# Second product of a two-layer FFN kernel: low part of the squares as stationary weights, in short 64-row pairs woven between the long passes, with five sum banks

## The chip, the cores and the metric

One core of a Trainium2 chip runs the whole problem. The metric is the device time of one execution in microseconds; less is better. The kernel before takes 2247.69 us (median of 2 runs, 2247.62 to 2247.77).

## The reference

A short dynamic convolution per head is followed by a squared-ReLU feed-forward layer. `x` is 8 x 4096 x 192, the heads are 8 of 24 columns, the convolution has 7 taps, the hidden width is 2048, and all arrays are float32 (the FFN's weights arrive as float64 and the kernel decodes them).

```python
w = softmax(weight_gen)                       # over the 7 taps
y = einsum('bshk,bskhg->bshg', w, x_unfolded) # 32768 tokens x 192
h = y @ w_in                                  # 192 x 2048
g = maximum(h, 0) ** 2
out = g @ w_out                               # 2048 x 192
```

## The kernel before

The 32768 tokens are cut into 64 chunks of 512 (`NCH`, 4 tokens for each of 128 partitions). For each chunk VectorE computes softmax and taps (L211, L216), transposes (L270), and DMAs over a DRAM scratch tile turn the result into `xT`, three groups of 64 rows, which stand twice, in partitions 0 to 63 and 64 to 127. ScalarE casts a high part `xh` (L235), VectorE subtracts it for the low part `xl` (L236). Both products use a split of each operand into a high and a low part in the round float format `F32R`; the product of the two low parts is left out.

The 2048 hidden columns are 16 blocks of 128, taken in pairs: a *step* `(c, j)` handles blocks 2j and 2j+1 of chunk c, 8 steps a chunk. In a step TensorE first makes the first product (`mm1`, L300): nine passes, each a *pair* of matmuls, one in rows 0 to 63 and one in rows 64 to 127 of the array, weights 64x128, 512 token columns moving, into two PSUM tiles `ph` of a pool of four. ScalarE then does relu (L316) and square (L320) of both blocks, and at the step's end casts their high parts `gh` (L324). VectorE subtracts for the low parts `gl` (L328) in the *next* step, ahead of that step's other VectorE work (the list `late`). TensorE's second product for a block pair (`mm2_turned`, L372) comes two steps after its first product (`LAG = 2`), behind the nine passes of that step: ten pairs, weights from `V` (the high and low parts of `w_out`), `gh` or `gl` moving with 512 columns, into four sum banks `acc` that hold the output turned: output columns on partitions, tokens along the free axis. The output's columns 0 to 127 use two banks, columns 128 to 191 the other two.

When a chunk's last block pair is summed, `sum_turned` (in step 1 of the next chunk) copies two banks on ScalarE (L380), adds the other two on VectorE (L382) and moves 64 rows by DMA (L383). `store_turned` turns the sums back: part 0 in step 5 (VectorE transpose L391, then 16 DMAs into `o_sb`, L400), part 1 in step 6 (an add L393, a transpose L394, 8 DMAs L400, then the store to DRAM, L405). All DMAs are issued on SyncE's queue, in program order.

The order of work on each engine is the order in which the code is written (`manual_schedule`); a table `todo` spreads the VectorE work of the next convolution over the steps, and the casts and low parts of the next chunk's `x` lie in step 6. The first chunk (c = 0) and the last have code of their own; in the last one `mm2` (L336, L345) uses the squares as weights, 128 tokens at a time. Chunks 1 to 62 go through `mm2_turned`.

Of the kernel before, what the change touches and what calls it, by code (L numbers as in the profile page):

```python
# [8 lines left out]
F32 = mybir.dt.float32  # L9
# [3 lines left out]
ALU = mybir.AluOpType  # L13
# [6 lines left out]
def kernel(  # L20
# [9 lines left out]
    nc = tc.nc  # L30
    B, S, D = x.shape
# [3 lines left out]
    P = 128  # L35
    Q = 32
# [3 lines left out]
    TC = 4  # L40
    NCH = n_chunks or R // TC
    TG = 8
    CPG = TG // TC
    NF = FF // P
    D1 = 64
    ND = D // D1
    N = TC * P
    NJ = NF // 2
    NU = NJ // 2
    WI = ND * P  # L50
    N_PE = 2
    LAG = 2
    CONV_BEG = 3
    OUT_STEP = 5
# [3 lines left out]
    stage = ctx.enter_context(tc.tile_pool(name="stage", bufs=3))  # L58
# [3 lines left out]
    gp = ctx.enter_context(tc.tile_pool(name="gp", bufs=NBUF))  # L62
    op = ctx.enter_context(tc.tile_pool(name="op", bufs=1))
    dram = ctx.enter_context(tc.tile_pool(name="dram", bufs=2, space=bass.MemoryType.DRAM))
    ps_h = ctx.enter_context(tc.tile_pool(name="ps_h", bufs=4, space=bass.MemoryType.PSUM))
    ps_o = ctx.enter_context(tc.tile_pool(name="ps_o", bufs=1, space=bass.MemoryType.PSUM))

    x_v = x.rearrange("b s d -> (b s) d").rearrange("(p r) d -> p r d", r=R)
# [1 line left out]
    out_v = out.rearrange("(p r) d -> p r d", r=R)  # L70
# [5 lines left out]
    W = const.tile([P, 2, NJ, WI], F32R, name="W")  # L76
    V = const.tile([P, NF, 2 * D], F32R, name="V")
# [207 lines left out]

    phs, rgs, ghs, gls, accs = {}, {}, {}, {}, {}

    def mm1(c, j, parts=(0, 1)):
        xh, xl = xts[c]["h"], xts[c]["l"]
        if 0 in parts:  # L290
            phs[c, 2 * j], phs[c, 2 * j + 1] = [ps_h.tile([P, N], F32, name="ph") for _ in range(2)]
        two = phs[c, 2 * j], phs[c, 2 * j + 1]
        seq = [(q, xx, k) for q, xx in ((0, xh), (0, xl), (1, xh)) for k in range(ND)]
        for n, (q, xx, k) in enumerate(seq):
            if q not in parts:
                continue
            for i in range(2):
                rows = slice(i * D1, (i + 1) * D1)
                w = W[rows, q, j, k * P:(k + 1) * P]
                nc.tensor.matmul(two[i], w, xx[rows, k], start=(n == 0), stop=(n == len(seq) - 1))  # L300

    def relu(c, fb):
        ph = phs.pop((c, fb))
# [14 lines left out]
    def square(c, fb):  # L318
        r = rgs[c, fb]
        nc.scalar.activation(r, r, AF.Square)  # L320
# [4 lines left out]

    def low(c, fb):
        gl = gls[c, fb] = gp.tile([P, N], F32R, name="gl")
        nc.vector.tensor_tensor(out=gl, in0=rgs.pop((c, fb)), in1=ghs[c, fb].bitcast(F32), op=ALU.subtract)  # L328

    def mm2_tile(c, fb, t):  # L330
        acc = accs[c][t]
# [23 lines left out]
            del ghs[c, fb], gls[c, fb]  # L355


    def mm2_turned(c, fb):
        if fb == 0:
            accs[c] = [ps_o.tile([P, N], F32, name=f"acc{t}") for t in range(4)]  # L360
        gh, gl = ghs.pop((c, fb)), gls.pop((c, fb))
        j, i = divmod(fb, 2)
        first, last = fb == 0, fb == NF - 1
        A, B = [(0, 0, gh), (0, 0, gl), (0, 1, gh)], [(2, None, gh), (2, None, gl)]
        seq = B + A if last or first else A + B
        for n, (b, q, g) in enumerate(seq):
            k = sum(1 for m in seq[:n] if m[0] == b)
            for h in range(2):
                rows = slice(h * D1, (h + 1) * D1)
                w = V[rows, fb, P:2 * P] if q is None else V[rows, fb, 2 * P * q:2 * P * q + P]  # L370
                fl = dict(start=first and k == 0, stop=last and k == (2 if b == 0 else 1))
                nc.tensor.matmul(accs[c][b + h], w, g[rows], **fl)  # L372

    works = {}

    def sum_turned(c):
        acc = accs[c]
        X = works[c] = stage.tile([P, 3, N], F32, name="raw")
        for k, b in ((1, 2), (0, 0)):
            nc.scalar.copy(X[:, k], acc[b])  # L380
        for k, b in ((1, 2), (0, 0)):
            nc.vector.tensor_tensor(out=X[:, k], in0=acc[b + 1], in1=X[:, k], op=ALU.add)  # L382
        nc.sync.dma_start(out=X[0:D1, 2], in_=X[D1:P, 1])  # L383

    def store_turned(c, part):
        X = works[c]
        if part == 0:
            o_sb = op.tile([P, TC, D], F32, name="o_sb", bufs=2)
            Y = stage.tile([P, 2, N], F32, name="raw")
            outs[c] = o_sb, Y  # L390
            nc.vector.transpose(Y[:, 0], X[:, 0])  # L391
        else:
            nc.vector.tensor_tensor(out=X[0:D1, 1], in0=X[0:D1, 1], in1=X[0:D1, 2], op=ALU.add)  # L393
            nc.vector.transpose(outs[c][1][0:D1, 1], X[0:D1, 1])  # L394
        o_sb, Y = outs[c]
        y = Y[:, part].rearrange("p (t q i) -> p q t i" if c < N_PE else "p (q t i) -> p q t i", t=TC, i=Q)
        for e in range(P // Q if part == 0 else D1 // Q):
            d0 = part * P + e * Q
            for q in range(P // Q):
                nc.sync.dma_start(  # L400
                    out=o_sb[q * Q:(q + 1) * Q, :, d0:d0 + Q],
                    in_=y[e * Q:(e + 1) * Q, q],
                )
        if part:
            nc.sync.dma_start(out=out_v[:, c * TC:(c + 1) * TC, :], in_=o_sb)  # L405

    outs = {}

# [43 lines left out]
    for u in range(NU):  # L452
# [11 lines left out]
        fbs = [4 * u + i for i in range(4)]  # L464
# [60 lines left out]
    for c in range(1, NCH):  # L525
        tail = c == NCH - 1
        for j in range(NJ):
            if j == 0 and c % 2 and (c + 3) // 2 * CPG < NCH:
                load_group((c + 3) // 2)
            if j == CONV_BEG and c + 2 < NCH:  # L530
                plan_conv(c + 2, *conv_steps(c + 2, 0))
            if c == 1 and j == 0:
                for t in range(TC):
                    finish(0, t)
                store(0, 0, TC)
            mm1(c, j)
            fbs = (2 * j, 2 * j + 1)
            done = None
            if len(pend) == LAG or tail and pend:
                c2, j2 = pend.pop(0)  # L540
                for fb in (2 * j2, 2 * j2 + 1):
                    mm2_turned(c2, fb)
                done = c2 if j2 == NJ - 1 else None
            for fb in fbs:
                relu(c, fb)
            for fb in fbs:
                square(c, fb)
            if not tail:
                pend.append((c, j))
            for f in late:  # L550
                f()
            late.clear()
            if done is not None:
                sum_turned(done)
            for f in todo.pop((c, j), []):
                f()
            if c > 1 and j == OUT_STEP:
                store_turned(c - 1, 0)
            if c > 1 and j == OUT_STEP + 1:
                store_turned(c - 1, 1)  # L560
            if not tail or j < NJ // 2:
                for fb in fbs:
                    high(c, fb)
                    late.append(lambda c=c, fb=fb: low(c, fb))
    c = NCH - 1
# [43 lines left out]
```

## Time and profile before

| | |
|---|---|
| runs | 2247.62 and 2247.77 us |
| span of the profiled execution | 2246.2 us |
| TensorE busy | 2228.7 us, 99% |
| weight loads busy | 1846.4 us, 82% |
| VectorE busy | 1877.6 us, 84% |
| ScalarE busy | 1797.6 us, 80% |
| GpSimd busy | 1.7 us |
| DMA | 191.78 MB, 85 GB/s |

In the profile, PE is TensorE's matmuls and PEld its weight loads, DVE is VectorE, ACT ScalarE, POOL GpSimd, SP or SPq the queue of SyncE that issues DMAs. A row of a timeline has the start in us, the time in us, engine, line, operation, output and inputs, shape, and in brackets how long the engine had been idle and what ended that. A row of a group has the count, the busy time, the mean of one in ns, and the idle time before. In the rows by windows each engine has busy us and, in brackets, its instructions, in the order PE, PEld, DVE, ACT, POOL; then come the granted TensorE clock, the DMA share and GB/s.

### The profile page before, as it was taken

The page shows a single profiled execution, that of the slowest core. Times are in us where ns is not written, and L with a number is a line of the kernel's source. Part 1 is how long each engine was busy: PE and PEld are TensorE (multiplying, and loading weights), DVE is VectorE, ACT ScalarE, POOL GpSimd, SP SyncE. Part 2 cuts the span into 40 slices and gives each one's busy share as a digit, 9 for nine tenths or more (in the row PEclk, how much of TensorE's full clock was granted, in tenths as well). Part 3 has the DMA queues.
Part 4 walks back from the last instruction along what each step waited for, and adds up shares of the span by engine and source line. Part 5 has one row for each costly group of instructions (what it writes and reads, how often), then busy time and mean ns, then how long its engine had stood idle before and what let it go on. Part 6 is the DMA issues. An engine that isn't in the chain of part 4 may idle for free.

```text
span 2246.2 us, 50242 instructions
## 1 busy us (share of the span) xinstructions
PE 2228.7 (99%) x19632; PEld 1846.4 (82%) x19632; DVE 1877.6 (84%) x2834; ACT 1797.6 (80%) x3462; POOL 1.7 (0%) x7
## 2 busy tenths in 40 slices
PE   7999999999999999999999999999999999999999
PEld 7788888888888888888888888888888888888887
DVE  8988888888888888888888888888888889888884
ACT  5688888888888888888888888888888888888876
POOL 0000000000000000000000000000000000000000
PEclk9999999999999999999999999999999999999999
DMA  5233233332333332333323333323333233332321
GB/s 170 60 91 90 58 99 85 91 100 67 80 94 81 100 88 59 99 84 93 99 54 93 88 88 99 83 65 100 84 91 90 57 99 86 91 99 71 76 66 45
DMA packets 321390, 191.78 MB, mean 85 GB/s; under 512 B 223752, under 2 KB 280968, under 8 KB 317184
## 3 DMA queue, kind: packets, MB, share of 16 engines
q1 hardware_dynamic: 321152, 188.58, 33.5%
q8 instruction: 153, 2.51, 0.5%
q14 instruction: 85, 0.70, 0.1%
HBM read 106.39 MB, written 49.55 MB: 69 GB/s over the span
## 4 chain that ended last, share of the span: by engine, by line
PE 97%; DVE 1%; ACT 1%; DMA 0%; issue 0%; SPq 0%; DVEq 0%; ACTq 0%
PE acc L372 49%; PE ph L300 45%; PE acc L336 1%; PE acc L345 1%; PE ph L253 1%; DVE pr L211 0%; DVE pr L216 0%; DMA xt<-in_x_dram 0%; ACT rg L320 0%; ACT gh L324 0%; DVE gl L328 0%; DMA raw<-in_moe_w_in_dram 0%; DVE V L156 0%; ACT rg L316 0%; ACT rg L310 0%
## 5 line engine op out<-in xcount | busy, mean ns | idle before, releaser
L372 PE MATMUL acc<-gh,V 64*128 64x512 f32 x5952 | 1007.5, 386 | 0.7 <-ACT gh L324 0.7
L300 PE MATMUL ph<-xh,W 64*128 64x512 f32 x6144 | 863.8, 386 | 2.0 <-ACT W L148 1.8
L316 ACT ACTIVATE rg<-ph 128x512 f32<-128x512 f32 x992 | 539.2, 597 | 346.9 <-PE ph L300 346.9
L372 PE MATMUL acc<-gl,V 64*128 64x512 f32 x3968 | 772.8, 386 | 1.0 <-DVE gl L328 1.0
L328 DVE TENSOR_TENSOR gl<-rg,gh 128x512 fp32r<-128x512 f32 x1008 | 644.4, 679 | 147.5 <-ACT gh L324 147.4
L300 PEld LDWEIGHTS ph<-xh,W 64*128 64x128 f32 x6144 | 575.8, 184 | 125.8 <-ACT W L148 3.0
L372 PEld LDWEIGHTS acc<-gh,V 64*128 64x128 f32 x5952 | 557.5, 184 | 118.1 <-ACT gh L324 1.1
L320 ACT ACTIVATE rg<-rg 128x512 f32<-128x512 f32 x1008 | 581.8, 634 | 0.0
L324 ACT CAST gh<-rg 128x512 fp32r<-128x512 f32 x1008 | 576.4, 627 | 2.6 <-PE acc L345 2.6
L372 PEld LDWEIGHTS acc<-gl,V 64*128 64x128 f32 x3968 | 371.7, 184 | 80.1 <-DVE gl L328 2.1
L300 PE MATMUL ph<-xl,W 64*128 64x512 f32 x3072 | 432.3, 386 | 0.0
L211 DVE TENSOR_TENSOR pr<-xt,wt 128x768 f32<-128x768 f32 x448 | 420.0, 950 | 3.4 <-DMA xt<-in_x_dram 1.2
L216 DVE TENSOR_TENSOR pr<-pr 128x768 f32<-128x768 f32 x381 | 361.5, 949 | 0.3
L300 PEld LDWEIGHTS ph<-xl,W 64*128 64x128 f32 x3072 | 288.3, 184 | 60.8 <-DVE xl L236 0.4
L236 DVE TENSOR_TENSOR xl<-xT,xh 128x512 fp32r<-128x512 f32 x186 | 117.7, 688 | 185.2 <-ACT xh L235 185.2
L235 ACT CAST xh<-xT 128x512 fp32r<-128x512 f32 x186 | 102.7, 625 | 0.0
L382 DVE TENSOR_TENSOR raw<-acc,raw 128x512 f32<-128x512 f32 x124 | 79.9, 686 | 3.0 <-ACT raw L380 3.0
L197 ACT ACTIVATE wt<-wt 128x224 f32<-128x224 f32 x64 | 25.0, 391 | 65.1 <-DVE wt L196 65.1
L380 ACT COPY raw<-acc 128x512 f32<-128x512 f32 x124 | 66.6, 598 | 0.0
L270 DVE STREAM_TRANSPOSE xr<-pr 128x768 f32<-128x768 f32 x62 | 60.7, 979 | 2.1
L394 DVE STREAM_TRANSPOSE raw<-raw 64x512 f32<-64x512 f32 x62 | 43.6, 704 | 2.1
L391 DVE STREAM_TRANSPOSE raw<-raw 128x512 f32<-128x512 f32 x62 | 43.7, 705 | 0.0
(46 smaller groups left out, 393.5 us busy)
## 6 DMA issues: line engine op xcount, KB each, us to landing
xT<-xd SPq DMA_DIRECT2D x124, 384.0 KB, 4.9
xt<-in_x_dram SPq DMA_DIRECT2D x31, 1344.0 KB, 7.0
out_dram<-o_sb SPq DMA_DIRECT2D x63, 384.0 KB, 2.7
xd<-xr SPq DMA_DIRECT2D x248, 96.0 KB, 2.0
o_sb<-raw SPq DMA_DIRECT2D x1488, 16.0 KB, 1.8
raw<-raw SPq DMA_DIRECT2D x62, 128.0 KB, 4.1
wt<-in_weight_gen_dram SPq DMA_DIRECT2D x31, 224.0 KB, 3.2
raw<-in_moe_w_in_dram SPq DMA_DIRECT2D x16, 192.0 KB, 4.1
```

What stands on the lines that cost most here:

```text
L211: tt(out=dst, in0=src, in1=wk.broadcast_to([P, n, G]), op=ALU.mult)
L216: tt(out=prs[k0], in0=prs[k0], in1=prs.pop(k), op=ALU.add)
L235: nc.scalar.copy(xh, src[k])
L236: tt(out=xl, in0=src[k], in1=xh.bitcast(F32), op=ALU.subtract)
L300: nc.tensor.matmul(two[i], w, xx[rows, k], start=(n == 0), stop=(n == len(seq) - 1))
L316: nc.scalar.activation(r, ph, AF.Relu)
L320: nc.scalar.activation(r, r, AF.Square)
L324: nc.scalar.copy(gh, rgs[c, fb])
L328: nc.vector.tensor_tensor(out=gl, in0=rgs.pop((c, fb)), in1=ghs[c, fb].bitcast(F32), op=ALU.subtract)
L372: nc.tensor.matmul(accs[c][b + h], w, g[rows], **fl)
L380: nc.scalar.copy(X[:, k], acc[b])
L382: nc.vector.tensor_tensor(out=X[:, k], in0=acc[b + 1], in1=X[:, k], op=ALU.add)
```

## The change

The second product of a block pair is now made of two kinds of pairs. Six *long* pairs keep `V` as weights and `gh` moving with 512 columns. The product of `gl` and the high part of `w_out` becomes eight *short* pairs: `gl` gives the weights, 128 tokens (64x128) at a time, and 192 columns of `V` move. Their sums are not turned (tokens on partitions) and get two banks of their own, `tx` and `ty`; the long pairs use three (`a0`, `a1`, `bb`). Five sum banks leave three for `ph`, in place of four; in the first chunk every second step takes the fifth sum bank for its second `ph` tile. The low parts are written with their tokens reordered so that blocks of 128 fit.

The short pairs are woven into the step's list of 15 long pairs (9 of the first product, 6 of the second): after the long passes number 2, 3, 5, 6, 10, 11, 13 and 14 (`SLOTS` has other places for a chunk's first and last block pair). Since the two row halves write the same banks at different times of a step, two orders per step are passed on through GpSimd: a no-op there waits for the one half's last matmul, and the other half's next matmul waits for the no-op.

The chunk's sum copies `tx` on VectorE and `a0`, `bb` and `ty` on ScalarE and needs one add less; the low sums are kept in `lows`. A third part of `store_turned`, in step 7, adds `lows` to `o_sb` on VectorE and then issues the store, which stood in part 1 before.

The places in the order of work. VectorE, from the transposes of step 6 to the low parts that step 0 of the next chunk makes (`gl` low parts, `pr` taps, `o_sb` the turned output), before:

```order
L394 STREAM_TRANSPOSE raw<-raw 64x512 [waits DVE_49]
L328 TENSOR_TENSOR gl<-rg,gh 128x512 [waits PE_49,Activation_49] x2
L211 TENSOR_TENSOR pr<-xt,wt 128x768
L216 TENSOR_TENSOR pr<-pr 128x768
L211 TENSOR_TENSOR pr<-xt,wt 128x768
L328 TENSOR_TENSOR gl<-rg,gh 128x512 [waits PE_49,Activation_49] x2
```

and now:

```order
L476 STREAM_TRANSPOSE raw<-raw 64x512 [waits DVE_49]
L341 TENSOR_TENSOR gl<-rg,gh 128x4x4x32 [waits PE_49,Activation_49] x2
L211 TENSOR_TENSOR pr<-xt,wt 128x768
L216 TENSOR_TENSOR pr<-pr 128x768
L211 TENSOR_TENSOR pr<-xt,wt 128x768
L466 TENSOR_TENSOR o_sb<-o_sb,lows 128x768 [waits DMAHW4_49,DMAHW5_49,DMAHW3_49,DMAHW6_49,DMAHW2_49,DMAHW7_49,DMAHW1_49,DMAHW0_49]
L341 TENSOR_TENSOR gl<-rg,gh 128x4x4x32 [waits PE_49,Activation_49] x2
```

The first pair of `gl` rows is block pair 6, the second block pair 7. The add of L466, which waits for DMAs, stands between them.

TensorE, in a chunk's step 1, which reads the low parts of the last chunk's block pair 7, before (the first product's passes, then the first rows of the second product; the numbers name the banks):

```order
L300 MATMUL ph<-xh,W 128x512 [waits Activation_49] x2
L300 MATMUL ph<-xh,W 128x512 x4
L300 MATMUL ph<-xl,W 128x512 x6
L300 MATMUL ph<-xh,W 128x512 x6
L372 MATMUL acc_15883<-gh,V 128x512 [waits Activation_49]
L372 MATMUL acc_15884<-gh,V 128x512
L372 MATMUL acc_15883<-gl,V 128x512 [waits DVE_49]
```

and now:

```order
L302 MATMUL ph<-xh,W 128x512 [waits Activation_49] x2
L302 MATMUL ph<-xh,W 128x512 x2
L423 MATMUL acc_17701<-V,gl 128x192 [waits DVE_49]
L423 MATMUL acc_17700<-V,gl 128x192
L302 MATMUL ph<-xh,W 128x512 x2
L423 MATMUL acc_17701<-V,gl 128x192
L423 MATMUL acc_17700<-V,gl 128x192
L302 MATMUL ph<-xl,W 128x512 x2
```

The first wait for VectorE's low part has moved from behind nine pairs of the first product to behind two; in the steps of block pairs 1 to 6 it stands behind three.

The diff:

```diff
--- before.py
+++ after.py
@@ -62,7 +62,7 @@
     gp = ctx.enter_context(tc.tile_pool(name="gp", bufs=NBUF))
     op = ctx.enter_context(tc.tile_pool(name="op", bufs=1))
     dram = ctx.enter_context(tc.tile_pool(name="dram", bufs=2, space=bass.MemoryType.DRAM))
-    ps_h = ctx.enter_context(tc.tile_pool(name="ps_h", bufs=4, space=bass.MemoryType.PSUM))
+    ps_h = ctx.enter_context(tc.tile_pool(name="ps_h", bufs=3, space=bass.MemoryType.PSUM))
     ps_o = ctx.enter_context(tc.tile_pool(name="ps_o", bufs=1, space=bass.MemoryType.PSUM))
 
     x_v = x.rearrange("b s d -> (b s) d").rearrange("(p r) d -> p r d", r=R)
@@ -285,19 +285,28 @@
 
     phs, rgs, ghs, gls, accs = {}, {}, {}, {}, {}
 
-    def mm1(c, j, parts=(0, 1)):
+    def mm1_passes(c, j, parts=(0, 1)):
         xh, xl = xts[c]["h"], xts[c]["l"]
         if 0 in parts:
-            phs[c, 2 * j], phs[c, 2 * j + 1] = [ps_h.tile([P, N], F32, name="ph") for _ in range(2)]
+            phs[c, 2 * j] = ps_h.tile([P, N], F32, name="ph")
+            phs[c, 2 * j + 1] = (ps_o.tile([P, N], F32, name="acc4") if c == 0 and j % 2
+                                 else ps_h.tile([P, N], F32, name="ph"))
         two = phs[c, 2 * j], phs[c, 2 * j + 1]
         seq = [(q, xx, k) for q, xx in ((0, xh), (0, xl), (1, xh)) for k in range(ND)]
-        for n, (q, xx, k) in enumerate(seq):
-            if q not in parts:
-                continue
-            for i in range(2):
-                rows = slice(i * D1, (i + 1) * D1)
-                w = W[rows, q, j, k * P:(k + 1) * P]
-                nc.tensor.matmul(two[i], w, xx[rows, k], start=(n == 0), stop=(n == len(seq) - 1))
+
+        def one(n, q, xx, k):
+            def f():
+                for i in range(2):
+                    rows = slice(i * D1, (i + 1) * D1)
+                    w = W[rows, q, j, k * P:(k + 1) * P]
+                    nc.tensor.matmul(two[i], w, xx[rows, k], start=(n == 0), stop=(n == len(seq) - 1))
+            return f
+
+        return [one(n, q, xx, k) for n, (q, xx, k) in enumerate(seq) if q in parts]
+
+    def mm1(c, j, parts=(0, 1)):
+        for f in mm1_passes(c, j, parts):
+            f()
 
     def relu(c, fb):
         ph = phs.pop((c, fb))
@@ -325,7 +334,11 @@
 
     def low(c, fb):
         gl = gls[c, fb] = gp.tile([P, N], F32R, name="gl")
-        nc.vector.tensor_tensor(out=gl, in0=rgs.pop((c, fb)), in1=ghs[c, fb].bitcast(F32), op=ALU.subtract)
+        ga, gb, to = rgs.pop((c, fb)), ghs[c, fb].bitcast(F32), gl
+        if N_PE <= c < NCH - 1:
+            ga, gb = [g.rearrange("p (q t j) -> p q t j", q=P // Q, j=Q) for g in (ga, gb)]
+            to = gl.rearrange("p (t q j) -> p q t j", q=P // Q, j=Q)
+        nc.vector.tensor_tensor(out=to, in0=ga, in1=gb, op=ALU.subtract)
 
     def mm2_tile(c, fb, t):
         acc = accs[c][t]
@@ -355,35 +368,104 @@
             del ghs[c, fb], gls[c, fb]
 
 
-    def mm2_turned(c, fb):
...
+    relay = {}
+
+    def waits_for(late_one, early_one):
+        tc.add_manual_dep(
+            late_one.ins, early_one.ins.name,
+            mybir.DependencyInfo(mybir.DependencyClass.Sync, mybir.DependencyReason.DATA),
+            reason="the other half of the rows has written this bank",
+        )
+
+    def passed_on(kind, last_one=None, next_one=None):
+        if last_one is not None:
+            relay[kind] = nc.gpsimd.engine_nop()
+            waits_for(relay[kind], last_one)
+        if next_one is not None:
+            waits_for(next_one, relay.pop(kind))
+
+    def mm2_passes(c, j):
+        if j == 0:
+            accs[c] = [ps_o.tile([P, N], F32, name=f"acc{b}") for b in range(5)]
+        a0, a1, bb, tx, ty = accs[c]
+        fbs = (2 * j, 2 * j + 1)
+        hs = [ghs.pop((c, fb)) for fb in fbs]
+        ls = [gls.pop((c, fb)) for fb in fbs]
+        turn = j % 2
+        last_b, last_t = [], []
+
+        def wide(kind, i):
+            fb, g = fbs[i], hs[i]
+            first, last = fb == 0, fb == NF - 1
+
+            def f():
+                to = {0: ((a0, 0), (bb, P)), 1: ((a0, 2 * P), (a1, 2 * P)), 2: ((bb, P), (a1, 0))}[kind]
+                for h, (b, col) in enumerate(to):
+                    rows = slice(h * D1, (h + 1) * D1)
+                    start = first and kind == (1 if b is a1 else 0)
+                    stop = last and kind == (1 if b is a1 else 0)
+                    m = nc.tensor.matmul(b, V[rows, fb, col:col + P], g[rows], start=start, stop=stop)
+                    if b is bb:
+                        last_b.append(m)
+                        if len(last_b) == 2:
+                            passed_on("side", last_one=m)
+                        if len(last_b) == 3:
+                            passed_on("side", next_one=m)
+            return f
+
+        def narrow(swap, i, t):
+            fb, g = fbs[i], ls[i]
+
+            def f():
+                for h in range(2):
+                    rows = slice(h * D1, (h + 1) * D1)
+                    b, tok = (tx, t) if h == swap else (ty, 2 + t)
+                    m = nc.tensor.matmul(
+                        b[:, t * D:(t + 1) * D], g[rows, tok * P:(tok + 1) * P], V[rows, fb, 0:D],
+                        start=fb == 0 and t == 0 and swap == 0, stop=fb == NF - 1 and t == 1 and swap == 0,
+                    )
+                    last_t.append(m)
+                    if len(last_t) == 8:
+                        passed_on("low", last_one=m)
+                    if len(last_t) == 9:
+                        passed_on("low", next_one=m)
+            return f
+
+        kinds, swaps = ((0, 1, 2), (0, 1)) if not turn else ((2, 1, 0), (1, 0))
+        return ([wide(k, i) for k in kinds for i in range(2)],
+                [narrow(w, i, t) for w in swaps for i in range(2) for t in range(2)])
+
+    SLOTS = {0: (9, 9, 10, 10, 13, 14, 14, 14), NJ - 1: (1, 2, 3, 4, 8, 9, 10, 11)}
+
+    def woven(wide, narrow, slots):
+        for n, f in enumerate(wide):
+            f()
+            for i, g in enumerate(narrow):
+                if slots[i] == n:
+                    g()
 
     works = {}
 
     def sum_turned(c):
-        acc = accs[c]
-        X = works[c] = stage.tile([P, 3, N], F32, name="raw")
-        for k, b in ((1, 2), (0, 0)):
-            nc.scalar.copy(X[:, k], acc[b])
-        for k, b in ((1, 2), (0, 0)):
-            nc.vector.tensor_tensor(out=X[:, k], in0=acc[b + 1], in1=X[:, k], op=ALU.add)
+        a0, a1, bb, tx, ty = accs[c]
+        X = stage.tile([P, 3, N], F32, name="raw")
+        L = op.tile([P, TC, D], F32, name="lows")
+        works[c] = X, L
+        lf = L.rearrange("p (b t) d -> p b (t d)", b=2)
+        nc.vector.tensor_copy(lf[:, 0], tx[:, 0:2 * D])
+        nc.scalar.copy(X[:, 0], a0)
+        nc.scalar.copy(X[:, 1], bb)
+        nc.scalar.copy(lf[:, 1], ty[:, 0:2 * D])
+        nc.vector.tensor_tensor(out=X[:, 0], in0=a1, in1=X[:, 0], op=ALU.add)
         nc.sync.dma_start(out=X[0:D1, 2], in_=X[D1:P, 1])
 
     def store_turned(c, part):
-        X = works[c]
+        X, L = works[c]
+        if part == 2:
+            o_sb, _ = outs[c]
+            nc.vector.tensor_tensor(out=o_sb, in0=o_sb, in1=L, op=ALU.add)
+            nc.sync.dma_start(out=out_v[:, c * TC:(c + 1) * TC, :], in_=o_sb)
+            return
         if part == 0:
             o_sb = op.tile([P, TC, D], F32, name="o_sb", bufs=2)
             Y = stage.tile([P, 2, N], F32, name="raw")
@@ -401,8 +483,6 @@
                     out=o_sb[q * Q:(q + 1) * Q, :, d0:d0 + Q],
                     in_=y[e * Q:(e + 1) * Q, q],
                 )
-        if part:
-            nc.sync.dma_start(out=out_v[:, c * TC:(c + 1) * TC, :], in_=o_sb)
 
     outs = {}
 
@@ -533,14 +613,17 @@
                 for t in range(TC):
                     finish(0, t)
                 store(0, 0, TC)
-            mm1(c, j)
             fbs = (2 * j, 2 * j + 1)
             done = None
+            first_product = mm1_passes(c, j)
             if len(pend) == LAG or tail and pend:
                 c2, j2 = pend.pop(0)
-                for fb in (2 * j2, 2 * j2 + 1):
-                    mm2_turned(c2, fb)
+                wide, narrow = mm2_passes(c2, j2)
+                woven(first_product + wide, narrow, SLOTS.get(j2, (2, 3, 5, 6, 10, 11, 13, 14)))
                 done = c2 if j2 == NJ - 1 else None
+            else:
+                for f in first_product:
+                    f()
             for fb in fbs:
                 relu(c, fb)
             for fb in fbs:
@@ -556,8 +639,8 @@
                 f()
             if c > 1 and j == OUT_STEP:
                 store_turned(c - 1, 0)
-            if c > 1 and j == OUT_STEP + 1:
-                store_turned(c - 1, 1)
+            if c > 1 and j in (OUT_STEP + 1, OUT_STEP + 2):
+                store_turned(c - 1, j - OUT_STEP)
             if not tail or j < NJ // 2:
                 for fb in fbs:
                     high(c, fb)
```

More of the change, by code (lines that the diff above doesn't have):

```diff
@@ L355, in mm2 @@
             del ghs[c, fb], gls[c, fb]
-    def mm2_turned(c, fb):
[L359 to L372, printed above, removed]
+    relay = {}
```

## The prediction

> **What bounds the kernel now.** I read the page first (engine shares, the chain that ended last), then the timelines of TensorE, VectorE, ScalarE and of the DMA queue over one chunk in the middle, then the last 25 us.
>
> ```profile
> span 2246.2 us, 50242 instructions
> PE 2228.7 (99%) x19632; PEld 1846.4 (82%) x19632; DVE 1877.6 (84%) x2834; ACT 1797.6 (80%) x3462; POOL 1.7 (0%) x7
> PE 97%; DVE 1%; ACT 1%; DMA 0%; issue 0%; SPq 0%; DVEq 0%; ACTq 0%
> ...
> L372 PE MATMUL acc<-gh,V 64*128 64x512 f32 x5952 | 1007.5, 386 | 0.7 <-ACT gh L324 0.7
> ...
> L372 PE MATMUL acc<-gl,V 64*128 64x512 f32 x3968 | 772.8, 386 | 1.0 <-DVE gl L328 1.0
> L328 DVE TENSOR_TENSOR gl<-rg,gh 128x512 fp32r<-128x512 f32 x1008 | 644.4, 679 | 147.5 <-ACT gh L324 147.4
> ```
>
> TensorE sets the time: it is busy 99% and holds 97% of the chain; for the low parts (`gl`, 679 ns each on VectorE) it waited 1.0 us in all. The next rows are one whole step of the pipeline (block pair 5 of a chunk; the next step begins at 1675.92).
>
> ```profile
> 1671.61 0.84 PE L300 MATMUL ph<-xh,W 64*128 64x512 f32 x6
> 1672.29 0.84 PE L300 MATMUL ph<-xl,W 64*128 64x512 f32 x6
> 1672.97 0.84 PE L300 MATMUL ph<-xh,W 64*128 64x512 f32 x6
> 1673.65 0.39 PE L372 MATMUL acc<-gh,V 64*128 64x512 f32 x2
> ...
> 1675.92 0.84 PE L300 MATMUL ph<-xh,W 64*128 64x512 f32 x6
> ```
>
> Six matmuls are three pairs of row halves and start 0.68 us apart, so a pair costs 0.227. A step is 9 + 10 = 19 pairs, 4.31 us; a chunk is 8 steps, 34.5 us. So the edit has two questions: what its own passes cost, and whether VectorE and the DMAs, idle or late at no cost today, still hand over in time.
>
> **Term 1, the passes: about nothing.** Per step four pairs of 512 columns go and eight pairs of 192 columns come: 15 long and 8 short. The columns alone would give 0.085 per short pair (192/512 of 0.227), a step of 4.09. But every short pair brings a new weight load. The tail of this kernel alternates 384 and 192 moving columns with a new load each time, though on the full array, and the place where TensorE once restarts shows what a load takes:
>
> ```profile
> 2229.99 0.25 PE L345 MATMUL acc<-V,gl 128*128 128x192 f32 x1
> 2230.08 0.36 PE L345 MATMUL acc<-V,gh 128*128 128x384 f32 x1
> 2230.28 0.25 PE L345 MATMUL acc<-V,gl 128*128 128x192 f32 x1
> 2230.36 0.36 PE L345 MATMUL acc<-V,gh 128*128 128x384 f32 x1
> ```
>
> ```profile
> 101.81 0.19 PEld L372 LDWEIGHTS acc<-gl,V 64*128 64x128 f32 x2 [0.83 <-DVE gl L328]
> 101.92 0.42 PEld L372 LDWEIGHTS acc<-gh,V 64*128 64x128 f32 x4
> ```
>
> A 384 and a 192 together take 0.285 (2229.99 to 2230.28, rounded rows); at the long pairs' rate the 384 is 0.170, which leaves 0.115 for the 192. At the restart the loads of both row halves go together (x2), and the next two follow 0.11 later: a pair's load occupies 0.11, hidden under a long pair (0.227), not under a short one (0.085). So a short pair costs 0.085 at best and 0.115 by the nearest row; I take 0.114. The step is 15 x 0.227 + 8 x 0.114 = 4.31: what four long passes free, eight loads take back. Bounds 4.09 and, if the halves' loads had to follow one another, 8 x 0.11 more, 5.2.
>
> **Term 2, the low parts come too late: this decides.** Before, a step's first read of a low part stood behind 9 + 1 pairs, 2.3 us into the step. Now it stands behind three pairs (0.68 us), and in the step with the chunk's last block pair behind two (0.45). The rows around the chunk's change, VectorE first, then TensorE's starts of the two steps that read the low parts of block pairs 6 and 7, then the DMA queue:
>
> ```profile
> 1675.58 0.70 DVE L391 STREAM_TRANSPOSE raw<-raw 128x512 f32<-128x512 f32 x1
> 1676.51 1.29 DVE L328 TENSOR_TENSOR gl<-rg,gh 128x512 fp32r<-128x512 f32 x2 [0.23 <-ACT gh L324]
> 1680.82 1.90 DVE L236 TENSOR_TENSOR xl<-xT,xh 128x512 fp32r<-128x512 f32 x3 [3.01 <-ACT xh L235]
> 1682.63 0.95 DVE L211 TENSOR_TENSOR pr<-xt,wt 128x768 f32<-128x768 f32 x1
> 1683.50 0.95 DVE L216 TENSOR_TENSOR pr<-pr 128x768 f32<-128x768 f32 x1
> ...
> 1685.72 1.24 DVE L328 TENSOR_TENSOR gl<-rg,gh 128x512 fp32r<-128x512 f32 x2
> 1686.88 0.94 DVE L211 TENSOR_TENSOR pr<-xt,wt 128x768 f32<-128x768 f32 x1
> ...
> 1688.62 0.94 DVE L211 TENSOR_TENSOR pr<-xt,wt 128x768 f32<-128x768 f32 x1
> 1689.49 1.28 DVE L328 TENSOR_TENSOR gl<-rg,gh 128x512 fp32r<-128x512 f32 x2
> ```
>
> ```profile
> 1684.53 0.84 PE L300 MATMUL ph<-xh,W 64*128 64x512 f32 x6
> 1688.84 0.84 PE L300 MATMUL ph<-xh,W 64*128 64x512 f32 x6
> ```
>
> ```profile
> 1676.31 16.44 SPq L400 DMA_DIRECT2D o_sb<-raw  x24
> 1694.05 0.36 SPq L405 DMA_DIRECT2D out_dram<-o_sb  x1
> ```
>
> Block pair 6: its first low part ends at 1685.72 + 0.68 = 1686.40 (679 ns). It hangs on TensorE: `xl` waited 3.01 us for the casts that follow the step's relu, and VectorE then never pauses. In the changed step four short pairs (4 x 0.114 = 0.46) stand ahead of the last pass that relu waits for, so it comes at 1686.86; with about 0.15 for the hand-over (0.04, below) and the load (0.11), 1687.01. TensorE could use it at 1684.53 + 0.68 = 1685.21. **It waits 1.8 us.**
>
> Block pair 7: the new add (o_sb += lows, VectorE, 128x768) stands in VectorE's order ahead of its low parts, behind the multiply of 1688.62. It needs all 24 transfers into o_sb, which the queue issues one after another. The store, which waits for the same transfers, was issued at 1694.05, 17.7 us after the first of them. So VectorE, which would be there at 1689.49, stands until 1694.05 + 0.46 (the transpose at 1675.58 hangs on relu too) = 1694.51. Then the add (0.87, the pitch of 1682.63 to 1683.50), the first low part (0.68), hand-over and load (0.15): 1696.21. TensorE could use it at 1688.84 + 0.45 = 1689.29. It is late by 6.9 us in all, and the 1.8 above is part of that: **1.8 in one step and 5.1 in the next.** Behind the add on VectorE wait both low parts of pair 7, the taps and the low parts of the new chunk; behind the short pass on TensorE, the rest of the first product, so relu and ScalarE too. VectorE then catches up: TensorE's halt gives it 6.9 us.
>
> What could move this: the landings.
>
> ```profile
> L400 SPq DMA_DIRECT2D o_sb<-raw x1488: 585/600/1967, 126.0 to 2235.6; - x186
> L405 SPq DMA_DIRECT2D out_dram<-o_sb x62: 357/362/363, 143.6 to 2237.6; - x62
> DMA to landing us min/median/max: 1.8/1.8/3.9
> ```
>
> Each issue takes 0.60 at the median and a landing 1.8 to 3.9; the 24 cannot be much shorter than 24 x 0.6, so I allow 0.5 less and 1.0 more per chunk.
>
> **Term 3, the clock after the halt.** A halt of 5.1 us is longer than any in the steady part. What TensorE's clock does then, the ends of the trace show:
>
> ```profile
> 9.80:12.06 2.26, 2.23 (x22) 2.26 (x24) 2.23 (x3) 0.23 (x1) 0.00 (x0) 1.00 1.12 231
> 12.06:15.47 3.41, 3.41 (x36) 3.41 (x34) 3.26 (x5) 1.00 (x2) 0.00 (x0) 1.00 1.10 275
> 15.47:20.00 4.53, 4.53 (x86) 4.53 (x84) 4.39 (x6) 1.41 (x3) 0.00 (x0) 1.00 0.83 175
> ...
> 2242.30:2244.40 2.10, 0.00 (x0) 0.00 (x0) 0.63 (x2) 0.44 (x1) 0.00 (x0) 0.98 0.18 65
> 2244.40:2246.20 1.80, 0.00 (x0) 0.00 (x0) 0.00 (x0) 0.00 (x0) 0.00 (x0) 0.50 0.23 83
> ```
>
> In the first column of counts, the matmuls of one kind run at 10.6 per us until 15.47 and at 19.0 after it: half pace for 5.7 us from the first at 9.8. At the end the granted clock falls to 0.50 some 2.1 us after the last matmul. A halt of 5.1 us is long enough for that, and the half pace then reaches into the steps behind it. Each us at half pace costs 0.5: nothing at the one end (the clock holds), 2.8 per chunk at the other (the 5.7 of the start). I take 2.3, nearer to the row. The start's row alone would give 2847. The Trainium skill (TensorE: Matmul & The Clock Gate, "What's actually happening") says that one idle window of about 3.4 us halves the clock and one busy window of that length restores it; by it the loss would be an estimated 1.7 per chunk and the sum 2780. The fall at the end agrees in kind, though it came after 2.1.
>
> **What is hidden.** ScalarE's third copy of the sums and the shift by 0.46, and three `ph` banks in place of four: before each step's relu ScalarE sits idle for 1.16, and relu starts 0.04 after the last pass (1672.97 + 0.84).
>
> ```profile
> 1673.85 1.09 ACT L316 ACTIVATE rg<-ph 128x512 f32<-128x512 f32 x2 [1.16 <-PE ph L300]
> ```
>
> With three banks a step's second tile needs the relu of the first block before: done at 2.24 + 0.46 + 0.6 = 3.3 of 4.31. If that 1.0 of cover went, each us beyond it would be paid per step. VectorE's copy of one bank replaces one add. GpSimd's no-op stands between two passes that are three long and two short pairs apart (0.91); less the end of the first (0.39) and the load (0.11), 0.41 are left for two hand-overs of 0.04 and the no-op. Beyond 0.41 a step pays, but in the two halting steps the wait swallows it: I take nothing, at most 1 us per chunk.
>
> **The sum.** The second product of the last chunk has its own code:
>
> ```profile
> L345 PE MATMUL acc<-V,gh x64: 333/358/440, 2223.7 to 2241.9; 128*128 128x384 f32 x64
> ```
>
> 61 chunks (2 to 62) have the add ahead of low parts that a later step reads: 61 x (6.9 + 2.3) = 561. Chunk 1 has only the wait on pair 6: 2. In the tail the add of chunk 62 holds the low parts of blocks 8 to 15 until the store's time, 2237.6, + 0.87 + 0.68 = 2239.2, where the second product wants the ninth block at 2223.7 + 8 x 1.14 (four of the 0.285 each) = 2232.9: 6. With the span 2246.2 that is 2815; the runs' median lies 1.5 above the span. **2817 us.**
>
> **Rivals.** *The clock holds* through the halt: 61 x 6.9 + 8 gives 2677. For it: nothing in the trace shows a halt of that length with work behind it, and the pause of 0.83 at 101.81 was followed by loads at the usual 0.23; against it, the fall 2.1 us after the end. *Only pair 6 is late*, because the transfers into o_sb land sooner than their queue shows: without that wait pair 7 is ready at 1689.49 + 0.46 + 0.87 + 0.68 + 0.15 = 1691.65, 0.6 after 1689.29 + 1.8, in all 2.4 per chunk, 61 x 2.4 + 2 = 148: 2396. Against it: 24 issues at 0.60. *Faster*: the short passes run at 0.085 to 0.093 and the low parts are in time; it decides from the add finding its transfers landed within 13.2 us of the transpose in place of 17.7, and pair 6 within 0.68 of its step. Then 496 steps save 0.16 to 0.22, 2140 to 2167. Only the column count speaks for it. *The row halves don't overlap* in short passes, or the no-op hop is slow: four steps of each chunk lie outside the waits, each 0.9 longer, 61 x 3.5 = 214 more, about 3030. Against it: the two loads that start together at 101.81.
>
> **Chances.** My sum 0.64, the clock holds 0.18, only pair 6 late 0.06, halves in turn or slow hop 0.07, faster 0.03, no change (the waits hidden, passes 0.114) 0.02. A measurement tells 2% from no change: faster 0.03, within 2% 0.02, slower 0.95. The range goes from the clock that holds with landings 0.5 sooner (2677 - 30, about 2650) to the full 2.8 with landings later by up to 1 (2847 + 61, about 2910).
>
> **What would show it.** Right: TensorE idle about 420 us in all, ended by VectorE's low parts, in two places of a chunk, about 1.8 and 5.1 long; VectorE idle about 4.6 per chunk ahead of the o_sb add, ended by DMA; granted clock below 1.00 in many of the slices; short pairs 0.11 apart from the next long one. Wrong: no DMA wait of VectorE at the add (then 2396 or less), the clock at 1.00 in all slices (2677), steps of 4.1 us or over 5 between the halts (the cost of the short passes), or waits on GpSimd.

## The result and the profile after

The changed kernel takes 2853.72 us (median of 2 runs, 2851.88 to 2855.55) against 2247.69 before: a ratio of 1.270, interval 1.268 to 1.272. The forecast was 2817 with a range of 2650 to 2910.

The page of the changed kernel (engine shares, the chain that ended last, the group of the short passes and that of the new add, each with its idle time and what ended it):

```profile
span 2853.8 us, 59114 instructions
PE 2457.0 (86%) x23600; PEld 2127.0 (75%) x23600; DVE 1934.4 (68%) x2896; ACT 1820.6 (64%) x3524; POOL 1.7 (0%) x7
...
PE 49%; SPq 23%; DVE 11%; issue 6%; ACT 6%; DMA 4%; DVEq 0%; ACTq 0%
PE ph L302 26%; SPq L482 23%; PE acc L407 13%; PE acc L423 9%; DMA o_sb<-raw 4%; DVE gl L341 4%; DVE pr L211 2%; ACT rg L325 2%; ACT rg L329 2%; DVE xl L236 2%; DVE pr L216 1%; DVE raw L473 1%; PE acc L349 1%; ACT gh L333 1%; DVE raw L475 1%
...
L423 PE MATMUL acc<-V,gl 64*128 64x192 f32 x7936 | 1076.8, 266 | 371.2 <-DVE gl L341 371.2
...
L466 DVE TENSOR_TENSOR o_sb<-o_sb,lows 128x768 f32<-128x768 f32 x62 | 59.4, 959 | 284.0 <-DMA o_sb<-raw 284.0
```

TensorE's share of the last chain has gone from 97% to 49%, and the queue that issues the 24 transfers into `o_sb` holds 23% of it. VectorE waited 284 us at the add, once in each of 62 chunks, and TensorE 371 us for low parts, where it had waited 1.0.

One chunk's change in the changed kernel, VectorE's timeline first, then the queue, then TensorE (the steps that read block pairs 6 and 7 begin at 1420.65 and 1426.69):

```profile
1422.23 1.24 DVE L341 TENSOR_TENSOR gl<-rg,gh 128x512 fp32r<-128x512 f32 x2
...
1425.14 0.94 DVE L211 TENSOR_TENSOR pr<-xt,wt 128x768 f32<-128x768 f32 x1
1429.92 0.96 DVE L466 TENSOR_TENSOR o_sb<-o_sb,lows 128x768 f32<-128x768 f32 x1 [3.83 <-DMA o_sb<-raw]
1430.79 1.29 DVE L341 TENSOR_TENSOR gl<-rg,gh 128x512 fp32r<-128x512 f32 x2
```

```profile
1412.68 15.90 SPq L482 DMA_DIRECT2D o_sb<-raw  x24
1430.90 0.36 SPq L467 DMA_DIRECT2D out_dram<-o_sb  x1
```

```profile
1420.65 0.91 PE L302 MATMUL ph<-xh,W 64*128 64x512 f32 x6
1422.93 0.35 PE L423 MATMUL acc<-V,gl 64*128 64x192 f32 x2 [1.38 <-DVE gl L341]
...
1426.69 0.65 PE L302 MATMUL ph<-xh,W 64*128 64x512 f32 x4
1431.53 0.53 PE L423 MATMUL acc<-V,gl 64*128 64x192 f32 x2 [4.19 <-DVE gl L341]
```

The first transfer is issued at 1412.68, the add starts at 1429.92, 17.2 later, with its 24 transfers landed; the low parts of block pair 7 follow it, and TensorE, two passes into the step, goes on at 1431.53. The short pass could have started 0.68 us into the first of the two steps and 0.45 into the second; over chunks 4 to 59 it started 1.58 and 4.92 later than that (medians of the starts in the trace; 1.60 and 4.39 in the chunk shown).

The clock, by windows around that halt (PE, PEld, DVE, ACT, POOL busy, each with its instructions; then the granted clock):

```profile
1420.00:1427.40 7.40, 5.97 (x60) 4.48 (x56) 6.05 (x9) 4.76 (x10) 0.00 (x0) 1.00 0.16 25
1427.40:1430.80 3.40, 0.00 (x0) 0.00 (x0) 0.88 (x2) 0.82 (x2) 0.00 (x0) 1.00 0.11 17
1430.80:1434.20 3.40, 2.67 (x16) 2.35 (x18) 3.40 (x6) 0.00 (x0) 0.00 (x0) 0.51 0.29 116
1434.20:1437.60 3.40, 3.40 (x22) 2.78 (x20) 0.82 (x2) 1.83 (x4) 0.00 (x0) 0.50 0.00 0
1437.60:1441.00 3.40, 3.40 (x36) 3.04 (x34) 2.35 (x4) 2.71 (x7) 0.00 (x0) 0.99 0.06 13
```

The clock falls about 3.5 us into this halt and stays at half for 6.8 us, most of it over the work behind the halt; over the whole run the mean granted clock is 0.927 (1.000 before).

### The profile page after: what moved, and what is told of

It is laid out like the page before. It is cut to its first block, busy times and chain, and to the rows that moved or that the text cites. A ratio compares the mean times of both kernels' runs of the same rounds, so it can differ in the third digit from the quotient of the medians.

```text
span 2853.8 us, 59114 instructions
## 1 busy us (share of the span) xinstructions
PE 2457.0 (86%) x23600; PEld 2127.0 (75%) x23600; DVE 1934.4 (68%) x2896; ACT 1820.6 (64%) x3524; POOL 1.7 (0%) x7
## 4 chain that ended last, share of the span: by engine, by line
PE 49%; SPq 23%; DVE 11%; issue 6%; ACT 6%; DMA 4%; DVEq 0%; ACTq 0%
PE ph L302 26%; SPq L482 23%; PE acc L407 13%; PE acc L423 9%; DMA o_sb<-raw 4%; DVE gl L341 4%; DVE pr L211 2%; ACT rg L325 2%; ACT rg L329 2%; DVE xl L236 2%; DVE pr L216 1%; DVE raw L473 1%; PE acc L349 1%; ACT gh L333 1%; DVE raw L475 1%
## 5 line engine op out<-in xcount | busy, mean ns | idle before, releaser
L423 PE MATMUL acc<-V,gl 64*128 64x192 f32 x7936 | 1076.8, 266 | 371.2 <-DVE gl L341 371.2
L423 PEld LDWEIGHTS acc<-V,gl 64*128 64x128 f32 x7936 | 859.7, 202 | 483.5 <-DVE gl L341 425.0
L302 PE MATMUL ph<-xh,W 64*128 64x512 f32 x6120 | 1021.4, 419 | 8.6 <-ACT rg L325 3.1
L407 PEld LDWEIGHTS acc<-gh,V 64*128 64x128 f32 x5952 | 580.8, 194 | 89.6
L302 PE MATMUL ph<-xl,W 64*128 64x512 f32 x3060 | 565.9, 437 | 0.0
L302 PEld LDWEIGHTS ph<-xl,W 64*128 64x128 f32 x3060 | 300.3, 202 | 47.0
L466 DVE TENSOR_TENSOR o_sb<-o_sb,lows 128x768 f32<-128x768 f32 x62 | 59.4, 959 | 284.0 <-DMA o_sb<-raw 284.0
L455 DVE COPY lows<-acc 128x384 f32<-128x384 f32 x62 | 34.6, 558 | 161.0 <-PE acc L423 161.0
L459 DVE TENSOR_TENSOR raw<-acc,raw 128x512 f32<-128x512 f32 x62 | 42.9, 692 | 49.6 <-ACT raw L456 49.6
L456 ACT COPY raw<-acc 128x512 f32<-128x512 f32 x62 | 36.4, 586 | 30.0 <-PE acc L407 29.6
```

The source lines that it names most:

```text
L407: m = nc.tensor.matmul(b, V[rows, fb, col:col + P], g[rows], start=start, stop=stop)
L423: m = nc.tensor.matmul(b[:, t * D:(t + 1) * D], g[rows, tok * P:(tok + 1) * P], V[rows, fb, 0:D], start=fb == 0 and t == 0 and swap == 0, ...
```

## The experiments

Theory A is that of the prediction: two hand-overs come late, the larger one because the add stands ahead of low parts and waits for 24 transfers, and the clock falls in that halt. Rival B: the added loads and passes cost the time, and the waits only follow. Rival C: short passes cost their columns, so the edit would gain once nothing waits.

**The transfers earlier.** Three steps earlier, the add where it was:

```diff
-    OUT_STEP = 5
+    OUT_STEP = 2
...
-            if c > 1 and j in (OUT_STEP + 1, OUT_STEP + 2):
-                store_turned(c - 1, j - OUT_STEP)
+            if c > 1 and j == OUT_STEP + 1:
+                store_turned(c - 1, 1)
+            if c > 1 and j == OUT_STEP + 5:
+                store_turned(c - 1, 2)
```

> The transposes and DMAs into o_sb of a chunk move from steps 5 and 6 to steps 2 and 3; the add of lows stays in step 7, so its 24 transfers have landed long before (about 17.7 us after step 2's transpose). Theory A (the add's DMA wait holds the low parts of block pair 7, and the clock drops after that halt): no DMA wait of VectorE at the add, no halt above 2 us, the clock at 1.00 in all slices, about 0.4 late at block pair 6 (VectorE has 1.4 us less to do ahead of it) and 0.6 at pair 7: 2310 to 2330 us. Rival B (the added weight loads and passes cost the time, with or without the wait, and take the clock down): 2750 or more.

Measured: 2391.79 us, mean clock 0.995. The waits of this kernel (who waited for whom, us in all, times, longest):

```profile
PEld acc L423 <- DVE gl L341: 135.0, 164, 3.1
...
PE acc L423 <- DVE gl L341: 71.7, 91, 2.7
DVE o_sb L466 <- DMA o_sb<-raw: 57.8, 42, 12.6
```

462 us of the 606 come back by moving no TensorE work, and the clock with them, so rival B falls. The size was missed by 60 to 80 us: the add still waits in 42 of 62 chunks, and the low parts of block pair 7 come 1.2 us late (median) in place of the expected 0.6. Rows of VectorE and of the queue show why the add waits:

```profile
1295.87 0.67 DVE L473 STREAM_TRANSPOSE raw<-raw 128x512 f32<-128x512 f32 x1
...
1319.90 0.96 DVE L466 TENSOR_TENSOR o_sb<-o_sb,lows 128x768 f32<-128x768 f32 x1 [1.23 <-DMA o_sb<-raw]
```

```profile
1295.97 1.79 SPq L276 DMA_DIRECT2D xd<-xr  x4
1299.40 1.29 SPq L281 DMA_DIRECT2D xT<-xd  x2
1300.80 16.32 SPq L482 DMA_DIRECT2D o_sb<-raw  x24
```

The transpose that feeds them ends at 1296.54, but in step 2 the transfers stand in the queue behind the next convolution's DMAs, of which `xT` waits for `xd` to land. They start at 1300.80, some 4 us behind the transpose, and the add starts 19.1 us later.

Short halts did not always leave the clock alone here. In seven places it fell behind idle times of TensorE of 1.7 to 2.7 us, while others of up to 2.3 us left it at 1.00. The pass that ends one of the seven, and the clock around it:

```profile
511.29 0.36 PE L423 MATMUL acc<-V,gl 64*128 64x192 f32 x2 [1.67 <-DVE gl L341]
```

```profile
509.60:511.90 2.30, 0.63 (x10) 0.57 (x10) 2.23 (x4) 0.93 (x2) 0.00 (x0) 1.00 0.17 64
511.90:515.30 3.40, 3.40 (x23) 2.91 (x22) 2.88 (x4) 0.30 (x1) 0.00 (x0) 0.50 1.07 379
515.30:518.70 3.40, 3.40 (x34) 2.87 (x34) 1.55 (x3) 3.40 (x8) 0.00 (x0) 0.99 0.42 171
```

**The short pairs late.** The add and its wait stay:

```diff
-    SLOTS = {0: (9, 9, 10, 10, 13, 14, 14, 14), NJ - 1: (1, 2, 3, 4, 8, 9, 10, 11)}
+    SLOTS = {}
...
-                woven(first_product + wide, narrow, SLOTS.get(j2, (2, 3, 5, 6, 10, 11, 13, 14)))
+                woven(first_product + wide, narrow, SLOTS.get(j2, (9, 9, 10, 10, 13, 14, 14, 14)))
```

> All steps place the short pairs as a chunk's first block pair does: behind long passes 9, 9, 10, 10, 13, 14, 14, 14, so the first low part is read 2.3 us into the step as before; the add with its DMA wait stays. Theory A: block pair 6 is no longer late (1.8 gone), the halt on pair 7 shrinks from 6.9 in all to about 4.4, relu is 0.46 sooner; with part of the half pace 2600 to 2680 us. Rival B (the places of the short pairs don't matter, the add alone decides): 2800 or more.

Measured: 2659.81 us, mean clock 0.955.

```profile
DVE o_sb L466 <- DMA o_sb<-raw: 295.1, 62, 16.5
PE acc L423 <- DVE gl L341: 262.4, 61, 6.0
```

TensorE now halts 61 times, once a chunk, by 4.3 us; the halt at block pair 6 is gone. The add's wait is as long as before. So the early places cost 194 us. They ask for the low parts sooner than VectorE makes them, and they also make the clock's loss larger. In this run a halt is in most cases followed by 3.4 us at half pace, in the changed kernel by twice that:

```profile
1337.80:1342.60 4.80, 0.72 (x9) 0.41 (x6) 2.09 (x4) 2.12 (x4) 0.00 (x0) 1.00 0.14 34
1342.60:1346.05 3.45, 3.45 (x24) 2.93 (x24) 3.01 (x5) 0.57 (x2) 0.00 (x0) 0.51 0.22 86
1346.05:1349.50 3.45, 3.45 (x36) 2.92 (x36) 3.44 (x5) 3.19 (x8) 0.00 (x0) 1.00 0.19 43
```

The half pace lasted 3.4 us after 53 halts here and 6.8 after 8; in the changed kernel it lasted 6.8 us 59 times and 3.4 four times. What separates the two is where the fall lies. Counted over the changed kernel and all its variants, without the fall at the kernel's end, the clock stayed at half for 6.8 us in the 68 cases in which it fell at least 0.46 us before the idle time of TensorE ended, and for 3.4 us in the 69 in which it fell later than that or behind the end. From the short pass that ends the halt to step 5 it takes 16.87 us here and 15.05 with the same places and no halt (the run with the add in the next chunk, below): the half pace costs 1.8 us a chunk.

**Both.**

> Both edits together: the o_sb transfers in steps 2 and 3, the short pairs behind long pass 9. Theory A: no halt is left on TensorE, VectorE's 24 transfers have landed; only the passes count, 15 long at 0.227 and 8 short at 0.113: a step of 4.31, about 2245 to 2255 us, no change from before; with 0.122 per short pair 2276. Rival B: 2700 or more. Rival C (the short pairs follow the columns, 0.085 to 0.093, once nothing waits): 2140 to 2170.

Measured: 2309.77 us, ratio 1.028 (1.026 to 1.030): above the expected 2245 to 2276. The add still waits, as in the run with the transfers earlier:

```profile
DVE o_sb L466 <- DMA o_sb<-raw: 110.2, 57, 11.5
...
PE acc L423 <- DVE gl L341: 19.9, 30, 1.6
```

The step that reads block pair 7 is 4.97 us long, all others 4.34 (medians over chunks 4 to 59). That this wait is the cause is shown by the run with the add in the next chunk, below.

**Useless work in the halt.** The changed kernel, with 20 pairs more:

```diff
+                if j2 == NJ - 1:
+                    for _ in range(20):
+                        for i in range(2):
+                            rows = slice(i * D1, (i + 1) * D1)
+                            nc.tensor.matmul(phs[c, 2 * j + i], W[rows, 0, j, 0:P], xts[c]["h"][rows, 0], start=True, stop=True)
                 woven(first_product + wide, narrow, SLOTS.get(j2, (2, 3, 5, 6, 10, 11, 13, 14)))
```

> The changed kernel with 20 useless pairs (the first pass of the first product, 512 columns, about 4.5 us) ahead of the step that reads block pair 7's low parts, where TensorE halts otherwise; the result is the same, since the real first pass starts the sums anew. Theory A (the halt has a length set by the DMAs, and the half pace after it comes from TensorE being idle): the useless work fits into the halt, the clock stays at 1.00, and the kernel with more work is faster by about 3 us a chunk: 2660 to 2690 us. Rival (the clock falls for another reason, as the load of eight more weight loads a step): 2850 or more.

Measured: 2715.74 us, 138 faster with 2480 matmuls more; mean clock 0.997. Its page and waits:

```profile
PE 2570.4 (95%) x26080; PEld 2153.5 (79%) x26080; DVE 1933.2 (71%) x2896; ACT 1818.1 (67%) x3524; POOL 1.7 (0%) x7
```

```profile
DVE o_sb L466 <- DMA o_sb<-raw: 303.2, 62, 16.5
...
PE acc L423 <- DVE gl L341: 118.2, 107, 2.4
```

VectorE waits for the DMAs as long as without them, so the halt's length isn't TensorE's doing; filling it keeps the clock. From the short pass that ends the halt to step 5 of the same chunk it takes 17.07 us here and 19.78 in the changed kernel (medians): the half pace costs 2.7 us a chunk. The time is 26 us above the expected upper end. The expected 3 us a chunk was too much by 0.3, and TensorE comes to the short pass that ends the halt 0.27 us later than in the changed kernel (11.66 us from the start of the step before it, against 11.40, medians); the add starts 0.16 us later behind the first transfer (17.92 against 17.76).

**The add in the next chunk.** As with both edits, but the add and the store move to step 0 of the next chunk, behind the low parts of block pair 7 and ahead of the sums that overwrite `lows`:

```diff
-            if c > 1 and j == OUT_STEP + 5:
-                store_turned(c - 1, 2)
+            if c > 2 and j == 0:
+                store_turned(c - 2, 2)
...
+    store_turned(c - 1, 2)
```

> As the run with both edits (transfers into o_sb in steps 2 and 3, short pairs behind long pass 9), but the add of lows and the store stand in step 0 of the next chunk, behind the low parts of block pair 7. In the run before the transfers started only behind the next convolution's DMAs and the add still waited 110 us in all. Theory A: no DMA wait of VectorE at the add, no halt on TensorE; every step is the 4.34 us that the undisturbed steps of that run show, 0.117 per short pair: 496 x 0.033 above before, 2262 to 2272 us. Rival C (the short pairs get cheaper once nothing waits, 0.113 or less): 2250 or less.

Measured: 2269.57 us, ratio 1.010 (1.008 to 1.011), as theory A expected. The new add and the short passes in this kernel:

```profile
L423 PE MATMUL acc<-V,gl 64*128 64x192 f32 x7936 | 979.0, 260 | 0.0
...
L466 DVE TENSOR_TENSOR o_sb<-o_sb,lows 128x768 f32<-128x768 f32 x62 | 58.8, 949 | 2.6 <-DMA o_sb<-raw 2.6
```

No halt is left, TensorE waits 0.0 for low parts, and the kernel is still 22 us slower than before. What remains is in the main the passes: every step takes 4.34 for 4.31, so 0.117 per short pair, 16 us over 61 chunks; the other 6 lie in the first chunks and the tail. Rival C falls. Between this run and the one with both edits only the place of the add and of the store differs: the 40 us between them are that wait.

**Half the columns.** Short pairs of 96 columns in that kernel:

```diff
-                        b[:, t * D:(t + 1) * D], g[rows, tok * P:(tok + 1) * P], V[rows, fb, 0:D],
+                        b[:, t * 96:(t + 1) * 96], g[rows, tok * P:(tok + 1) * P], V[rows, fb, 0:96],
...
```

The copies out of the sums, which the cut above leaves out, write the 96 columns twice.

> The kernel with the add in the next chunk and the short pairs late, but each short pair moves 96 columns of w_out in place of 192, so half of the low parts' product is left out (the sums' second half repeats the first); loads, waits and everything else stay. If a short pair costs its weight load (0.11 or more), the time doesn't move: within 10 us of the run with 192 columns. If it costs its columns, 8 x 0.04 less per step, about 150 us less.

Measured: 2280.51 us: 11 more, not 150 less. Every step takes 4.36 in place of 4.34 (medians); why it takes more with fewer columns stays open.

```profile
L423 PE MATMUL acc<-V,gl 64*128 64x96 f32 x7936 | 983.9, 237 | 0.0
```

Half the columns save nothing, so a short pair's price is not that of its columns. The loads, as many as before and 0.11 each by the prediction's row of the restart, would account for it; but no run changes the loads alone, and a fixed price of every pass is not ruled out. The Trainium skill (TensorE: Matmul & The Clock Gate, "LDWEIGHTS (loading the stationary operand)") states that a load's time goes by its columns alone, an estimated 0.107 for 128; the 0.113 to 0.122 of this case's runs lie a little above that.

**The short pairs at the change's places, with a step more.**

```diff
-    LAG = 2
+    LAG = 3
...
-    OUT_STEP = 5
+    OUT_STEP = 3
...
```

The add and the store move as in the run with the add in the next chunk.

> The short pairs at the places of the change (alternating with long ones, from long pass 2 on), the add of lows in step 0 of the next chunk, the transfers into o_sb from step 3, and the second product three steps behind the first in place of two, so the low parts have a step more. Theory A: the early places cost nothing but passes once the low parts have time: no wait of TensorE for VectorE above 30 us in all, steps of 4.38 as the undisturbed steps of the change show: 2280 to 2300 us. Rival (the weaving itself brings the halts, by relu and ScalarE): 2350 or more.

Measured: 2289.34 us, as theory A expected. The short passes' idle time is 0.0:

```profile
L423 PE MATMUL acc<-V,gl 64*128 64x192 f32 x7936 | 1515.2, 250 | 0.0
```

So weaving as such brings no halt. A step takes 4.38 here, 0.122 per short pair between long ones. That price is not fixed: in the run with the transfers earlier, of the 224 steps 4 to 7 of chunks 4 to 59, 115 took 4.31 us and 108 took 4.38, with the same work at the same places; in the run with useless work it was 90 and 133, and in the changed kernel all but 4 took 4.38. What puts a chunk into the one or the other is not shown.

## Why the prediction was right

- *The passes, about nothing.* Right in kind: 15 long and 8 short pairs are no gain. Mis-sized by a little: in the changed kernel a short pair took 0.122 and not 0.114, so a step 4.38 and not 4.31, 0.56 us a chunk, 34 us in all. The forecast's 4.31 is the other length that the woven steps have, in the run with the transfers earlier in half of them. One sign that was named did not come: the next long pair does not start 0.11 behind a short one but 0.088, about the time of its columns (0.085). The rest shows one pair later: the long pair behind a short one holds the array for 0.255 us in place of 0.227, so the short pair is paid for by its neighbour (medians in the changed kernel):

```profile
1425.35 0.25 PE L423 MATMUL acc<-V,gl 64*128 64x192 f32 x2
1425.43 0.42 PE L407 MATMUL acc<-gh,V 64*128 64x512 f32 x2
1425.69 0.25 PE L423 MATMUL acc<-V,gl 64*128 64x192 f32 x2
```

- *Block pair 6 late by 1.8.* Measured 1.58. The short pairs late took this halt away.
- *Block pair 7 late by 5.1 more, behind the add's DMA wait.* Measured 4.92. The shift by relu was right: the first transfer is issued 5.15 us into step 5 (median), 4.70 before, 0.45 later for the 0.46 of the sum. VectorE's wait at the add was forecast at 4.6 a chunk and is 284 us in 62 chunks, 4.6. TensorE idle for low parts was forecast at about 420 us and is 371: the two delays are together 0.4 us a chunk shorter than forecast, and in each of the two steps the pairs ahead end some 0.2 us behind the point from which the delay counts, by the rows above. With the transfers earlier, the short pairs late and the add behind the low parts, no halt is left; no run moves the add alone in the changed kernel.
- *The clock.* It fell, as the likeliest case had it, and costs 2.7 a chunk for the 2.3 taken, near the 2.8 of the start's row. Useless work in the halt took the fall away and left VectorE's wait. That the size came out so close is in part luck. The 2.3 was chosen between 0 and 2.8 and not worked out, and the start is no halt: with the short pairs late, halts of 4.3 us cost 1.8. (The start's rows have 1.00 in the column of the clock at half pace, since the trace's clock record begins only at 15.42; the pace is read from the counts, and the first of the three rows gives 9.7 per us, not 10.6.) By the rule of the Trainium skill (TensorE: Matmul & The Clock Gate, "What's actually happening") one busy window of about 3.4 us restores the clock, an estimated loss of 1.7 a chunk. The run with the short pairs late agrees (3.4 us, 1.8); in the changed kernel the clock falls while TensorE still idles for about 1 us, so the 3.4 us behind the fall are not all busy, and the half pace lasts 6.8.
- *The sum.* Per chunk 1.58 + 4.92 + 2.7 + 0.56 = 9.76, times 61 is 595; the 608 between the spans leave some 12 for the first chunks and the tail. The forecast had 9.2 a chunk: its two delays were together 0.4 too long, its clock term 0.4 and its passes 0.56 too short.
- *What was hidden* stayed hidden: three `ph` banks and ScalarE's third copy show little wait on TensorE. GpSimd's no-ops have no rows of their own, but TensorE has no idle time that they could explain: 0.0 us ahead of the long passes of the second product, and ahead of the short ones the waits for low parts alone.

```profile
L407 PE MATMUL acc<-gh,V 64*128 64x512 f32 x5952 | 1002.0, 416 | 0.0
```

```profile
PE ph L302 <- ACT rg L325: 3.1, 3, 2.0
```

Of the rivals, the held clock (2677) is close to the run with useless work (2716), which makes its condition true. That the case in which only pair 6 is late (2396) is close to the run with early transfers (2392) is chance: there the delays are 0.4 at pair 6 and 1.2 at pair 7. What the 0.01 between a load's 0.11 and the short pair's 0.117 to 0.122 is stays open; the steps of 4.31, 0.113 per short pair, show that it can be absent.

## What to carry to other kernels

An instruction that waits on DMAs holds everything behind it in its engine's order, here 284 us of VectorE's time: before putting one ahead of work that the bound engine needs, read when the queue lands its last transfer, not how long one takes. Before making a pass shorter, set its columns against the load of its weights: here 96 columns took no less time than 192 with the same loads. And when an operand is read earlier in a step, the time at which it is ready in the profile of before tells the new wait to within a few tenths of a microsecond.

## What the runs showed of the hardware

The halt costs more than its length: a halt of about 5 us brought the granted clock to 0.50 for 6.8 us, and 20 useless pairs in the halt made the kernel 138 us faster. The clock's record has a grid: in the eight runs of the changed kernel and its variants, every stretch between two changes of the clock is a multiple of 3.413 us (6.83 is two of them, the 37.55 at full pace between two halts of the changed kernel eleven). The half pace lasted one such unit when TensorE was back at work at the fall, or within 0.3 us of it, and two when it idled on for 0.46 us or more. How long TensorE idles does not alone decide whether the clock falls: 1.67 us brought it down in the run with the transfers earlier, 3.51 us near the start of the run with a step more left it at 1.00, and all 61 halts above 4 us in the changed kernel brought it down. The eight more loads of a step did not touch the clock: it was 0.999 in the run with the add in the next chunk. And passes of 192 columns between passes of 512, all with new weights, took 0.113 or 0.122 us for the same code, steady over many steps.
